# An attention-decode backward kernel: dV written over V, one buffer for dK, V loaded one turn earlier

## The chip, the cores and the metric

The kernel runs on one core of one Trainium2 chip. The metric is device time in microseconds (us) for one execution, the median of several runs; lower is better. The profile is one execution recorded by the hardware profiler. Its engines are PE (TensorE matmul; PEld is its weight load), DVE (VectorE), ACT (ScalarE), POOL (GpSimd) and SP (SyncE, which here only issues DMA transfers). L645 is line 645 of the kernel.

## What is computed

The reference mixes two branches by a gate and returns the output and the gradients of nine inputs. Almost all bytes belong to the first branch, one decode step of attention with 32 heads, 4096 cached keys and a head size of 128:

```python
q = (x @ wq).reshape(B, Sq, H, Dh).transpose(0, 2, 1, 3)
scores = einsum("bhqd,bhkd->bhqk", q, k_cache) * Dh ** -0.5
o = einsum("bhqk,bhkd->bhqd", softmax(scores), v_cache)
a = o.transpose(0, 2, 1, 3).reshape(B, Sq, H * Dh) @ wo
h = einsum("bsd,df->bsf", x, w1) + b1          # second branch
b = einsum("bsf,fd->bsd", h * tanh(softplus(h)), w2)
out = g * a + (1 - g) * b                      # g = sigmoid(sum(x * gate_w))
```

With one query per head, dV of a head is the outer product of its probabilities and of dO, and dK the outer product of dscores and of q. So K and V (33.6 MB each, bf16) are read once, and dK and dV, as large, are written once. wq, wo, w1, w2 and their gradients are much smaller.

## The kernel before

Two heads make a pair; there are NP = 16 pairs and 8 groups of two pairs. One pair's K, V, dK or dV is one tile of 128 partitions x 64 rows x 128 values in bf16, 2048 KB, 16 KB in each partition. Buffers hold 2 K tiles and 2 V tiles (pool `kv_in`) and 2 output tiles `o_sb` (pool `outs`), which dV and dK share in turn.

The main loop (L882 to L974) makes turn i, for i = 0 to 14; turn 15 stands behind it, written out. The order of instructions is written by hand, each engine runs its own list in that order, and waits between engines follow from the tiles' uses, by the parts of a tile that are touched. Turn i does two things, interleaved:

- *Outputs of pair i.* `softmax` (a PE transpose to `mx`, L610, and a maximum), `exps` on ACT (L620), `pjs` on DVE (L624), a small PE product with the sums (`zd_mm`, L628), `probs` on DVE (L632 to L642: p, ds, and their masked copies pm, dsm). Then `dq_o` (L681) has PE read K(i) and V(i) for dq and o. `dv_out` and `dk_out` write dV(i) and dK(i) in four quarters each on DVE (L645, `outer`); the store is issued on SP's queue after the last quarter (L666), or in halves in turns 0 and 15 (L664).
- *Scores of pair i+1.* PE transposes K(i+1) and V(i+1) in eight pieces each (`k_pe`, `v_pe`, L549), ACT copies each piece out of PSUM (`ev`, L560), PE multiplies by q and dO (`k_rows`, `v_rows`, L575), and `rw_cp` (L586), `x_tr` (L592), `sels` (L599) and `maxes` (L604, L606) bring the scores into the form that the next turn's softmax reads. `k_pe(i + 1, 0)` to `(i + 1, 2)` stand ahead of `zd_mm(i)` in PE's list.

SP issues in its list's order, and an issue that has to wait holds up those behind it. In turn i these are: K(i+2) and V(i+2) right after `dq_o(i)` (L917, L918); dV(i)'s store; in odd turns weights for a later group (L935, L937); in even turns the stores of dwo and dwq of the group before (L424, L415); dK(i)'s store. A load waits until the tile that last used its buffer has been read.

Other work is put between these steps by `side(at, i, g, hp)` at named places `do("mx")`, `do("e")` and so on. In even turns (hp = 0) it does the sums of the group before: `f_diag` (DVE, L329 and L310), `f_o4` and `f_bc` (PE, L339 and L316), `l_pe` (L388), `l_add` (L394), `f_dx` (DVE, L400) and `f_dwq` (DVE, L410) for three columns at "dv" and two at "dk0", and `f_dwo` (ACT, L418). `mlp` puts in pieces of the second branch. In turn 14 dK is written into a free `Kn` buffer, in turn 15 dV into a free `Vn` buffer (L655, L657). After turn 15's outputs DVE, PE and ACT make three rows of small outputs (`vec_rows`, L1043), which POOL stores.

Of the kernel before, what the change touches and what calls it, by code (L numbers as in the profile page):

```python
# [16 lines left out]
def kernel(  # L17
# [25 lines left out]
    P = 128  # L43
# [45 lines left out]
    out9_rows = out_9.rearrange("(c p) -> c p", p=P)  # L89

    const = ctx.enter_context(tc.tile_pool(name="const", bufs=1))
    KBUFS, VBUFS = 2, 2
    kv_in = ctx.enter_context(tc.tile_pool(name="kv_in", bufs=KBUFS))
    kvT = ctx.enter_context(tc.tile_pool(name="kvT", bufs=1))
    outs = ctx.enter_context(tc.tile_pool(name="outs", bufs=2))
    wts = ctx.enter_context(tc.tile_pool(name="wts", bufs=3))
    grp_sb = ctx.enter_context(tc.tile_pool(name="grp_sb", bufs=2))
    small = ctx.enter_context(tc.tile_pool(name="small", bufs=3))
# [6 lines left out]

    def load(tiles, src, name, i, parts=1):
        if i < NP:
            tiles[i] = kv_in.tile([P, J, Dh], BF16, name=name, tag=name)
            for k in range(parts):
                yield nc.sync.dma_start(tiles[i][:, k * J // parts:(k + 1) * J // parts, :],  # L110
                                        src[i][:, k * J // parts:(k + 1) * J // parts, :])
# [4 lines left out]
    def load_v(i):  # L116
        return list(load(vts, Vv, "Vn", i))
# [6 lines left out]
    def load_wqp(k):  # L124
        a, z = WQP[k]
        wqp[k] = wts.tile([P, RC, (z - a) * GD], BF16, name="wq_p", tag="wq_p", bufs=2)
        for g in range(a, z):
            wqs[g] = wqp[k][:, :, (g - a) * GD:(g - a + 1) * GD]
        nc.sync.dma_start(wqp[k][:], wq_v[:, :, a * GD:z * GD])
# [20 lines left out]
    load_v(1)  # L150
    w1_sb = const.tile([P, RC, F], BF16, name="w1_sb")
    nc.sync.dma_start(w1_sb[:], w1_v)
    load_wqp(1)
    load_wo(2)
    w2_sb = const.tile([P, FCN, D], BF16, name="w2_sb")
# [235 lines left out]
    def l_add(g, slot, o):  # L391
        ax = groups[g]["ax"]
        if o:
            nc.vector.tensor_tensor(aT_acc[:], aT_acc[:], ax[:, 0, :], ALU.add)  # L394
        if ("q", g) in wT:
            nc.vector.tensor_copy(dx_parts[:, :, slot], ax[:, 1, :])
# [26 lines left out]
    def f_dwo_st(g):  # L423
        nc.sync.dma_start(dwo4_v[g], wos[g][:])  # L424
# [227 lines left out]
    def out_part(w, i, dst, col4, row, k):  # L652
        if k == 0:
            if w == "k" and i == NP - 2:
                o_t[w, i] = kv_in.tile([P, J, Dh], BF16, name="Kn", tag="Kn")  # L655
            elif w == "v" and i == NP - 1:
                o_t[w, i] = kv_in.tile([P, J, Dh], BF16, name="Vn", tag="Vn")  # L657
            else:
                o_t[w, i] = outs.tile([P, J, Dh], BF16, name="o_sb", tag="o_sb")
        outer(o_t[w, i], col4, row[:, i % 2 * Dh:(i % 2 + 1) * Dh], k * JQ, (k + 1) * JQ)  # L660
        if i in (0, NP - 1):
            if k % 2:
                js = slice((k - 1) * JQ, (k + 1) * JQ)
                nc.sync.dma_start(dst[i][:, js, :], o_t[w, i][:, js, :])  # L664
        elif k == 3:
            nc.sync.dma_start(dst[i], o_t.pop((w, i))[:])  # L666

    def dv_out(i, k):
        out_part("v", i, dVv, p4s[i], groups[i // 2]["do_row"], k)
# [3 lines left out]
            out_part("k", i, dKv, ds4s[i], groups[i // 2]["qs_row"], k)  # L673

    def dq_o(i):
        K, V = kts.pop(i), vts.pop(i)
        for r in range(J // 8):
            for c in range(4):
                N, m = (K, dsmb) if c < 2 else (V, pmb)
                jb = 4 * (2 * r + c % 2)  # L680
                nc.tensor.matmul(rw[32 * c:32 * c + 8, :], lhsT=m[:, jb:jb + 4, :].rearrange("p q a -> p (q a)"),  # L681
                                 rhs=N[:, jb:jb + 4, :].rearrange("p j d -> p (j d)"),
                                 start=(i == NP - 1 and r == 0), stop=(i == NP - 1 and r == J // 8 - 1))
# [132 lines left out]
    def side(at, i, g, hp):  # L816
        nx, pv = g + 1 < NG, g > 0
        if hp == 0 and pv:
            f = g - 1
            if at == "probs":  # L820
                f_new(f)
                f_diag(f)
            if at == "dqo":
                f_o4(f)
                f_bc(f)
                f_o4c(f)
            if at in ("v2", "v3", "v4", "v5"):
                f_dwo(f, int(at[1]) - 2)
            if at == "k7":
                l_pe(f, 0, G)  # L830
            if at == "v5":
                f_dwo_st(f)
            if at == "dv":
                l_add(f, f, True)
                for c in range(3):
                    f_dx(f, c)
                    f_dwq(f, c)
            if at == "dk0":
                for c in range(3, RC):
                    f_dx(f, c)  # L840
                    f_dwq(f, c)
                f_dwq_st(f)
        if hp == 0:
            kind, gw = ("o", g + 1) if nx else ("q", g)
            if at == "v3":
                w_pe(kind, gw, 0)
                ev()
            if at == "vr":
                w_pe(kind, gw, 1)
                ev()  # L850
            if at == "v7":
                w_pe(kind, gw, 2)
                ev()
        if hp == 0 and nx:
            if at == "v7":
                g_new(g + 1)
                g_q(g + 1)
            if at == "x":
                g_qcol(g + 1)
                g_do(g + 1)  # L860
        if hp == 1 and nx:
            if at == "mx":
                g_qpair(g + 1)
            if at == "k1":
                g_qpair_cp(g + 1)
                g_docol(g + 1)
            if at == "k3":
                g_dopair(g + 1)
            if at == "dv":
                g_qs(g + 1)  # L870
            if at == "probs":
                g_dopair_cp(g + 1)
        if hp == 1 and at in ("dv", "v3", "dk0"):
            mlp(i, 2.0)
        elif at == "e" or hp == 1 and at == "k3":
            mlp(i, 1.0, ("act", "dh", "dx", "dw1"))
        elif at == ("v7", "dk1")[hp]:
            mlp(i, 0.9 + 0.9 * hp, ("h", "b1", "b", "diag", "bc"))
        if i >= 1 and at in (("k7", "v2", "v3", "v4", "v5", "v7") if hp == 1 else ("k7", "v7")):
            dw2_some(1)  # L880

    for i in range(NP - 1):  # L882
        g, hp = i // 2, i % 2

        def do(at):
            side(at, i, g, hp)

        if i == NP - 2:
            assert not mq
            nc.sync.dma_start(dw1_v[:, 0:3, :], w1_sb[:, 0:3, :])  # L890
            nc.sync.dma_start(dw1_v[:, 3:RC, :], w1_sb[:, 3:RC, :])
        mx, negM = softmax(i)
        do("mx")
        k_pe(i + 1, 0)
        k_pe(i + 1, 1)
        ev()
        dqo_red(i - 1, xs[i])
        exps(i, negM)
        do("e")
        ev()  # L900
        do("k1")
        k_pe(i + 1, 2)
        ev()
        pjs(i)
        zd_mm(i, mx)
        k_pe(i + 1, 3)
        ev()
        do("k3")
        probs(i, mx)
        do("probs")  # L910
        k_pe(i + 1, 4)
        k_pe(i + 1, 5)
        k_rows(i + 1, 0)
        ev()
        ev()
        dq_o(i)
        load_k(i + 2)  # L917
        load_v(i + 2)  # L918
        if i == NP - 2:
            assert dw2_next[0] == FCN  # L920
            m_dw2(0)
            dw2_store()
            nc.gpsimd.dma_start(db1_row, dh_bc[0:1, :])
        do("dqo")
        dv_out(i, 0)
        dv_out(i, 1)
        k_pe(i + 1, 6)
        ev()
        k_pe(i + 1, 7)
        ev()  # L930
        do("k7")
        dv_out(i, 2)
        dv_out(i, 3)
        if hp == 1 and 0 < g and g + 2 < NG:
            load_wo(g + 2)  # L935
        if hp == 1 and g % 2 == 0 and g > 0 and g + 4 <= NG:
            load_wqp(g // 2 + 1)  # L937
        do("dv")
        v_pe(i + 1, 0)
        v_pe(i + 1, 1)  # L940
        k_rows(i + 1, 1)
        ev()
        ev()
        v_pe(i + 1, 2)
        ev()
        do("v2")
        v_pe(i + 1, 3)
        ev()
        do("v3")
        v_pe(i + 1, 4)  # L950
        v_pe(i + 1, 5)
        v_rows(i + 1, 0)
        ev()
        do("v4")
        ev()
        do("vr")
        dk_out(i, 0)
        do("dk0")
        v_pe(i + 1, 6)
        ev()  # L960
        do("v5")
        v_pe(i + 1, 7)
        ev()
        do("v7")
        dk_out(i, 1)
        do("dk1")
        v_rows(i + 1, 1)
        rw_cp(i + 1)
        x_tr(i + 1)
        dk_out(i, 2)  # L970
        dk_out(i, 3)
        sels(i + 1)
        maxes(i + 1)
        do("x")  # L974
# [102 lines left out]
```

## Time and profile before

| | |
|---|---|
| median of 3 runs | 404.15 us (403.64 to 405.39) |
| the profiled execution | 403.98 us, of which 402.2 us from the first to the last instruction (the span) |
| DVE, PE, ACT busy | 279.4, 292.4, 226.2 us (69%, 73%, 56% of the span) |
| bytes moved | 164.54 MB, half read and half written |
| K's loads, issue to landing, median | 13.7 us |
| V's loads, issue to landing, median | 18.3 us |
| stores of o_sb, issue to landing, median | 16.6 us |

In the profile's groups of instructions the columns are: line, engine, operation, tiles, shapes and count, then busy us, mean ns of one, idle us just before them and what ended it. The slices cut the span in 40 equal parts; a digit is the busy share in tenths. The lists in order of time give the start, the length, the engine and the line.

### The profile page before, as it was taken

What the parts mean: (1) busy time and instruction counts of PE and PEld (TensorE: products, weight loads), DVE (VectorE), ACT (ScalarE), POOL (GpSimd) and SP (SyncE); (2) the same over time, 40 slices, a digit from 0 to 9 for tenths busy, and PEclk for the clock granted to TensorE, in tenths of its full rate; (3) what the DMA queues carried; (4) which work ended last, traced back from release to release, by engine and by line L of the source; (5) the groups of instructions that cost most, each with busy time, mean ns of one, the idle gap of its engine ahead of it and who ended that gap; (6) DMA issues with size and microseconds to landing.
All of it is one profiled execution on the core that took longest, in us unless ns stands there. A gap on an engine that the chain in (4) does not pass through costs nothing.

```text
span 402.2 us, 7414 instructions
## 1 busy us (share of the span) xinstructions
PE 292.4 (73%) x2886; PEld 207.5 (52%) x2886; DVE 279.4 (69%) x696; ACT 226.2 (56%) x484; POOL 25.5 (6%) x50
## 2 busy tenths in 40 slices
PE   3788888886968696984939886695967879197530
PEld 3557654665645474754627563553735655074320
DVE  2206537587966996478798956767496897859890
ACT  3464756485557544583535858377486885168130
POOL 9200005100000000000000004000000000010001
PEclk9898999898999888797977999599698999779555
DMA  7999999999999999999999999999999999999996
GB/s 273 432 423 413 416 420 431 424 427 423 403 402 425 432 419 424 404 429 430 424 433 400 380 408 431 428 423 425 418 406 383 419 376 427 433 417 430 412 407 234
DMA packets 20115, 164.54 MB, mean 409 GB/s; under 512 B 2455, under 2 KB 2456, under 8 KB 10904
## 3 DMA queue, kind: packets, MB, share of 16 engines
q1 hardware_dynamic: 18960, 159.62, 96.1%
q0 software_dynamic: 1088, 4.44, 2.7%
q8 instruction: 22, 0.36, 0.3%
q14 instruction: 13, 0.11, 0.1%
q10 hardware_dynamic: 32, 0.01, 0.0%
HBM read 82.44 MB, written 82.44 MB: 410 GB/s over the span
## 4 chain that ended last, share of the span: by engine, by line
DMA 62%; DVE 26%; PE 6%; issue 2%; ACT 2%; POOL 0%; POOLq 0%; DVEq 0%; ACTq 0%
DMA out_dram<-o_sb 60%; DVE o_sb L645 18%; PE tr L549 3%; DVE junk L400 2%; DMA Kn<-in_A_k_cache_dram 1%; DVE Kn L645 1%; DVE Vn L645 1%; DVE wq_p L410 1%; ACT T L560 1%; PE rw L575 1%; DVE ds L637 0%; PE q_ps L246 0%; PE mx L610 0%; DVE wo_g L421 0%; PE do_ps L301 0%
## 5 line engine op out<-in xcount | busy, mean ns | idle before, releaser
L560 ACT COPY T<-tr 128x512 f32<-128x512 f32 x256 | 140.9, 592 | 115.8 <-PE tr L549 67.6
L549 PE MATMUL tr<-ident_f,Kn 128*128 128x128 f32 x512 | 89.9, 338 | 7.6 <-DMA Kn<-in_A_k_cache_dram 7.6
L645 DVE TENSOR_TENSOR o_sb<-do_row,p 128x2048 bf16<-128x2048 bf16 x60 | 69.5, 1220 | 32.1 <-DMA out_dram<-o_sb 32.1
L549 PE MATMUL tr<-ident_f,Vn 128*128 128x128 f32 x512 | 77.2, 284 | 12.6 <-ACT T L560 12.6
L549 PEld LDWEIGHTS tr<-ident_f,Kn 128*128 128x128 f32 x512 | 78.4, 181 | 14.0 <-issue 9.8
L645 DVE TENSOR_TENSOR o_sb<-qs_row,ds 128x2048 bf16<-128x2048 bf16 x60 | 71.3, 1235 | 11.5 <-DMA out_dram<-o_sb 11.5
L549 PEld LDWEIGHTS tr<-ident_f,Vn 128*128 128x128 f32 x512 | 54.1, 140 | 37.1 <-ACT T L560 22.8
L610 PE MATMUL mx<-ident_f,m_s 128*128 128x128 f32 x16 | 6.8, 427 | 36.9 <-DVE m_s L606 36.9
L681 PE MATMUL rw<-Kn,dsm 128*8 128x512 bf16 x256 | 31.9, 394 | 1.2 <-DVE dsm L641 1.1
L681 PE MATMUL rw<-Vn,pm 128*8 128x512 bf16 x256 | 31.9, 394 | 0.0
L575 PE MATMUL rw<-T,doz 128*32 128x512 bf16 x256 | 20.3, 392 | 14.3 <-ACT T L560 14.3
L400 DVE SCALAR_TENSOR_TENSOR junk<-wq_p,dq_bc 128x512 bf16<-128x512 bf16 x35 | 24.0, 685 | 0.0
L610 PEld LDWEIGHTS mx<-ident_f,m_s 128*128 128x128 f32 x16 | 2.7, 167 | 41.2 <-DVE m_s L606 41.2
L418 ACT ACTIVATE wo_g<-da_bc,o 128x640 bf16<-128x640 bf16 x28 | 23.8, 849 | 0.0
L592 PE MATMUL x<-ident_f,rw_sb 128*128 128x128 f32 x68 | 12.2, 306 | 13.7 <-ACT rw_sb L586 13.7
L575 PE MATMUL rw<-T,qz 128*32 128x512 bf16 x256 | 20.8, 400 | 0.4 <-ACT T L560 0.4
L592 PEld LDWEIGHTS x<-ident_f,rw_sb 128*128 128x128 f32 x68 | 7.7, 149 | 22.8 <-ACT rw_sb L586 22.8
L681 PEld LDWEIGHTS <-dsm 128*8 128x8 bf16 x256 | 11.5, 88 | 14.0 <-DVE dsm L641 2.5
L604 DVE TENSOR_REDUCE m<-sd 128x1 f32<-128x64 f32 x16 | 3.4, 215 | 18.0 <-ACT sd L599 18.0
L586 ACT COPY rw_sb<-rw 128x512 f32<-128x512 f32 x17 | 10.0, 590 | 10.4 <-PE rw L575 5.6
L575 PEld LDWEIGHTS <-doz 128*32 128x32 bf16 x256 | 5.4, 94 | 19.6 <-issue 19.4
L599 ACT COPY sd<-x 64x128 f32<-64x128 f32 x32 | 8.3, 260 | 12.7 <-PE x L592 7.3
(183 smaller groups left out, 358.5 us busy)
## 6 DMA issues: line engine op xcount, KB each, us to landing
out_dram<-o_sb SPq DMA_DIRECT2D x27, 2048.0 KB, 16.6
Kn<-in_A_k_cache_dram SPq DMA_DIRECT2D x15, 2048.0 KB, 13.7
Vn<-in_A_v_cache_dram SPq DMA_DIRECT2D x15, 2048.0 KB, 18.3
out_dram<-o_sb SPq DMA_DIRECT2D x6, 1024.0 KB, 13.5
wq_p<-in_A_wq_dram SPq DMA_DIRECT2D x4, 1280.0 KB, 24.9
wo_g<-in_A_wo_dram SPq DMA_DIRECT2D x8, 640.0 KB, 21.0
out_dram<-wo_g SPq DMA_DIRECT2D x8, 640.0 KB, 13.2
out_dram<-wq_p SPq DMA_DIRECT2D x4, 1280.0 KB, 14.7
```

The source lines that it names most:

```text
L400: nc.vector.scalar_tensor_tensor(jq[:], in0=wqs[g][:, c, :], scalar=1.0, in1=groups[g]["dq_bc"][:], op0=ALU.mult, op1=ALU.mult, accum_out= ...
L410: nc.vector.tensor_scalar(wqs[g][:, c, cs], groups[g]["dq_bc"][:, cs], x_col_f[:, c:c + 1], None, ALU.mult)
L418: nc.scalar.activation(wos[g][:, hh, :], da_bc[:], ACT.Copy, scale=groups[g]["o4"][:, hh:hh + 1])
L549: nc.tensor.transpose(tp[:, t, :], words[:, t * P:(t + 1) * P], ident_f[:])
L560: nc.scalar.copy(TT[w, i, k][:, (3 - c) * (TB // 2):(4 - c) * (TB // 2), :], tp[:])
L575: nc.tensor.matmul(rw[32 * c:32 * (c + 1), :], lhsT=z[:, at:at + 32], rhs=Tb[:, c, par, :, :], start=first and par == 0, stop=last and par ...
L586: nc.scalar.copy(rw_sb[i][:].rearrange("p t r -> p (t r)"), rw[:])
L592: nc.tensor.transpose(xs[i][:, 3 - j, :], t[:, j, :], ident_f[:])
L599: nc.scalar.copy(sd[i][hs].rearrange("p s (k j) -> p k s j", k=2), v[hs, :, 8 + 4 * a:12 + 4 * a].rearrange("p j (k s) -> p k s j", k=2))
L610: nc.tensor.transpose(mx[:, 0:P], dgms.pop(i)[:].to_broadcast([P, P]), ident_f[:])
L645: nc.vector.tensor_tensor(dst[:, a:b, :].rearrange("p j (k t) -> p j k t", t=4), row.rearrange("p (k t) -> p k t", t=4).unsqueeze(1).to_br ...
L681: nc.tensor.matmul(rw[32 * c:32 * c + 8, :], lhsT=m[:, jb:jb + 4, :].rearrange("p q a -> p (q a)"), rhs=N[:, jb:jb + 4, :].rearrange("p j ...
```

## The change

Three V buffers instead of two, one `o_sb` buffer instead of two. dV(i) is written into V(i)'s own tile and stored from there; `o_sb` is left to dK (in turn 14 a Kn buffer, as before). V(i+3) instead of V(i+2) is loaded in turn i, at its end behind dK's store; V(2) is loaded in the prologue. In even turns the group's `f_diag` moves from "probs" to "e", `f_o4` and `f_bc` from "dqo" to "k3"; the place "dv" (three columns of `f_dx` and `f_dwq`, `g_qs`, and `mlp` in odd turns) moves ahead of `dv_out`, `l_add` gets a place of its own, "la", and "dk0" moves ahead of dK's first quarter. `mlp`'s small pieces swap places "e" and "k3".

```diff
-    KBUFS, VBUFS = 2, 2
+    KBUFS, VBUFS = 2, 3
...
-    outs = ctx.enter_context(tc.tile_pool(name="outs", bufs=2))
+    outs = ctx.enter_context(tc.tile_pool(name="outs", bufs=1))
...
-            tiles[i] = kv_in.tile([P, J, Dh], BF16, name=name, tag=name)
+            tiles[i] = kv_in.tile([P, J, Dh], BF16, name=name, tag=name, bufs=KBUFS if name == "Kn" else VBUFS)
...
     nc.sync.dma_start(w1_sb[:], w1_v)
+    load_v(2)
     load_wqp(1)
...
             if w == "k" and i == NP - 2:
-                o_t[w, i] = kv_in.tile([P, J, Dh], BF16, name="Kn", tag="Kn")
-            elif w == "v" and i == NP - 1:
-                o_t[w, i] = kv_in.tile([P, J, Dh], BF16, name="Vn", tag="Vn")
+                o_t[w, i] = kv_in.tile([P, J, Dh], BF16, name="Kn", tag="Kn", bufs=KBUFS)
+            elif w == "v":
+                o_t[w, i] = vts.pop(i)
             else:
                 o_t[w, i] = outs.tile([P, J, Dh], BF16, name="o_sb", tag="o_sb")
...
     def dq_o(i):
-        K, V = kts.pop(i), vts.pop(i)
+        K, V = kts.pop(i), vts[i]
...
-            if at == "probs":
+            if at == "e":
                 f_new(f)
                 f_diag(f)
-            if at == "dqo":
+            if at == "k3":
                 f_o4(f)
                 f_bc(f)
                 f_o4c(f)
...
+            if at == "la":
+                l_add(f, f, True)
             if at == "dv":
-                l_add(f, f, True)
                 for c in range(3):
                     f_dx(f, c)
                     f_dwq(f, c)
...
-        elif at == "e" or hp == 1 and at == "k3":
+        elif at == "k3" or hp == 1 and at == "e":
             mlp(i, 1.0, ("act", "dh", "dx", "dw1"))
...
         dq_o(i)
         load_k(i + 2)
-        load_v(i + 2)
...
         do("dqo")
+        do("dv")
         dv_out(i, 0)
         dv_out(i, 1)
...
-        do("dv")
+        do("la")
         v_pe(i + 1, 0)
...
         do("vr")
+        do("dk0")
         dk_out(i, 0)
-        do("dk0")
...
         dk_out(i, 3)
+        load_v(i + 3)
         sels(i + 1)
         maxes(i + 1)
```

## The prediction, made before the changed kernel was run

> **What bounds the kernel.** I read the page's slices first, then the waits, then time-ordered lists of the last three turns. A turn i is one pass of the main loop: the softmax and the outputs of pair i, and the transposes of pair i+1.
>
> From the page:
> ```profile
> DMA  7999999999999999999999999999999999999996
> GB/s 273 432 423 413 416 420 431 424 427 423 403 402 425 432 419 424 404 429 430 424 433 400 380 408 431 428 423 425 418 406 383 419 376 427 433 417 430 412 407 234
> DMA packets 20115, 164.54 MB, mean 409 GB/s; under 512 B 2455, under 2 KB 2456, under 8 KB 10904
> ```
> All slices but the first and last have the DMA engines busy 90% or more, and all but three of those move 400 to 433 GB/s. 164.54 MB at 430 GB/s are 382.7 us of a 402.2 us span. The 19.5 us of difference lie at the ends (270 GB/s in the first 10 us: 3.7; the last 12 us, at 321 and less: 4.7), in rates just under 430, and in dips: the 10 us stretches from 100, 110, 220, 230, 290, 300 and 320 moved 400, 402, 398, 374, 406, 369 and 385 GB/s, together 6.4 us short of 430. In the dips the engines are still busy:
> ```profile
> 230.00:240.00 10.00, 8.15 (x100) 5.47 (x97) 5.52 (x23) 6.78 (x18) 0.00 (x0) 1.00 0.95 374
> 300.00:310.00 10.00, 6.02 (x45) 4.95 (x45) 6.81 (x18) 6.80 (x15) 0.00 (x0) 0.83 0.99 369
> 380.00:390.00 10.00, 5.52 (x63) 3.21 (x53) 9.97 (x21) 3.22 (x9) 0.00 (x0) 0.50 0.95 396
> ```
> (The last two columns are the busy share and GB/s; the columns in front are PE, PEld, DVE, ACT, POOL and PE's clock.) A share of 0.99 at 369 GB/s means slow packets, not a lack of work. So DVE's waits for stores cost little:
> ```profile
> L645 DVE TENSOR_TENSOR o_sb<-do_row,p 128x2048 bf16<-128x2048 bf16 x60 | 69.5, 1220 | 32.1 <-DMA out_dram<-o_sb 32.1
> L645 DVE TENSOR_TENSOR o_sb<-qs_row,ds 128x2048 bf16<-128x2048 bf16 x60 | 71.3, 1235 | 11.5 <-DMA out_dram<-o_sb 11.5
> ```
> DVE stands still because the queue ahead of it is full; the chain of waits gives `out_dram<-o_sb` 60% for the same reason. **DMA is the bound in the middle, and only at the end does computing catch up with it.**
>
> The Trainium skill, HBM Reference, Specifications, says that a core streaming alone reaches about 425 GB/s and is bounded by its DMA engines. By that the bytes need 387.2 us instead of 382.7, with 15 us around them instead of 19.5; the trace passes it (439 GB/s in 340 to 350), and either way the rule speaks against a gain from fewer waits.
>
> **The change, part by part.** Bytes and DMA counts stay as they are: 16 loads each of K and V, the same stores. DVE, ACT and PE run the same instructions.
>
> *dV in V's buffer.* DVE no longer waits for an older store before dV: the 32.1 us go. What is late next in a turn is K. V(i+2) now stands in front of K(i+2) instead of behind it. A 2048 KB transfer takes 4.9 us (K(15) landed 15.6 us after its issue at 334.56, V(15) 20.0 after 334.99: 350.1 and 355.0). So K(i+2) lands 4.9 us later against the same stream of bytes. PE's transposes of K stand ahead of the small product for the softmax's sums (L628), so a late K holds back the probabilities and all behind them. I expect every turn from the second on to start its PE work when K lands.
>
> *Does DMA then run dry?* Count from k, the landing of the K that turn j transposes, by distances of turn 14 (first transpose 352.25, probabilities done 357.2, Kn's and Vn's reads done about 359.4). Turn j issues K(j+2) at k+7.3, dV(j) at about k+12.7 (4.9 to the probabilities, 3.0 of group sums, 4.6 of dV), dK(j) at k+20.7 or before. The queue after k holds dV(j-1) 4.9, weights 1.5 to 4.6, dK(j-1) 4.9, V(j+2) 4.9: 16.2 us before K(j+2) is needed, 21.1 before dV(j), 27.5 before dK(j). Margins: 8.9, 8.4, 6.8 us. V(j+2) has to wait on SP until dV(j-1), whose buffer it takes, has landed at k+4.9; 6.4 us are then still queued. Queued on SP behind that wait are K's load and dV's store, both later anyway. An issue costs at most 3.0 us before its data flow (first load: 1024 KB issued at 0.81, landed 5.40 later, 2.4 of it the transfer). **Cost in the middle: 0**, and the cover is those margins of 3.4 us and more.
>
> SP's own waits in the profile show where such a wait is spent: SP stood 80.8 us before loads of line 110 until PE had read the buffer (line 681). The Trainium skill, DMA: Bandwidth & Descriptors, Anatomy of one DMA, says the same in general: DMA engines wait for no semaphore, the sequencer that issues does. By that V's wait holds up everything that SP issues next, which is the third rival below; by the margins it costs nothing.
>
> *One buffer for dK.* dK(j) may start when dK(j-1) has landed, k+11.3 to k+14.4; DVE reaches it at k+13 to k+16. Nothing to a few tenths; covered by the 6.8 us. The last one, dK(15), comes two turns after the buffer was last used and doesn't wait.
>
> *Group sums in the softmax.* The 3.0 us of sums (three pairs of 0.62 and 0.35 us in the chain) now stand before dV instead of after it, in even turns: dV is later, dK not. The two small PE products (o_ps and bc_ps, 0.46 us in all behind dq_o) go ahead of the probabilities: up to 0.5 us gained in the PE chain of an even turn.
>
> *V(2) in the first loads.* K(2) lands 4.9 us later; in the first 60 us the queue only gets fuller (K(2) was issued at 38.8 and the loads before it landed until 47.3). 0.
>
> **The end is another matter.** After K(15) no load is left, and the stores of turn 15 depend on a chain from K(15)'s transposes to the last small outputs:
> ```profile
> 352.25 2.77 PE L549 MATMUL tr<-ident_f,Kn 128*128 128x128 f32 x12
> ...
> 374.81 0.47 PE L610 MATMUL mx<-ident_f,m_s 128*128 128x128 f32 x1 [1.46 <-DVE m_s L606]
> ...
> 379.43 0.64 PE L681 MATMUL rw<-Vn,pm 128*8 128x512 bf16 x2
> ```
> ```profile
> 373.39 0.53 ACT L599 COPY sd<-x 64x128 f32<-64x128 f32 x2 [0.74 <-PE x L592]
> ```
> ```profile
> 378.91 1.22 DVE L645 TENSOR_TENSOR Vn<-do_row,p 128x2048 bf16<-128x2048 bf16 x1
> ```
> ```profile
> SPq L1072 <- DMA out_dram<-vec_rows: 5.2, 1, 5.2
> ```
> 1. *K(15).* Its landing moves from 350.1 to V(15)'s old place, 355.0, and the transposes from 352.25 to about 355.15: +2.9. The chain to `sd` (ends 373.9) is PE and ACT, nearly without slack; less the 0.5 above, +2.4 (bounds: 0, if the chain has slack that I don't see, to 2.9).
> 2. *dV(15).* It was written into a free Vn buffer at 378.91, while PE still read V(15). Now it is V(15)'s own: DVE must wait until PE has read that quarter. Stores of parts of o_sb are issued while DVE writes the next part (39.73, with DVE working to 45.6), so waits go by parts; the first quarter's last read ends at 380.07: +1.2 (all of V: 382.6, +3.7). In earlier turns this wait falls under the group sums or where DMA has margin.
> 3. *Last outputs.* SP's last long wait is for the three small stores of `vec_rows`, issued at 394.15 to 395.49 and landed 5.0 us later (median), with 2 us to the span's end. They hang on DVE's last chain and move by all of 1 and 2. I take back 0.4, since they then meet less traffic (bounds 0 to 0.7, the median's 5.0 against the 5.7 of the first one). The large stores have some 2 us of room of their own (the first half of dK(15) landed 5.7 us after its issue, 2.4 of it transfer, and at most 3.0 around it), so they end before that.
>
> Sum: 2.4 + 1.2 - 0.4 = **+3.2**, on the profiled execution's 403.98 (span 402.2, 1.8 around it): **407.2 us**. The median of the runs, 404.15, is 0.2 above that execution; I don't add it. By the bounds: 0 + 1.2 - 0.7 = +0.5 to 2.9 + 3.7 = +6.6, so 404.5 to 410.6.
>
> **Rivals.**
> - *The end is absorbed, 404 to 405 (0.25).* Dips and the chain's slack vary; if K(15) comes early against the computing, step 1 is 0 and step 2 is hidden by large stores that end last anyway (+0.5). For it: 0.5 us lie between the two ends now. Against: PE's waits in that turn, 0.1 to 1.3 us each, are for ACT, which was itself busy.
> - *Store waits were the bound, 399 (0.15).* If the dips come from the order of loads and stores, new order may end them: 6.4 us less, with the end's 3.2 still paid or not: 397.6 to 400.8. For it: the chain's 60%. Against: busy share 0.99 in the dips; loads and stores still alternate in pairs.
> - *SP's wait starves the queue, 410 (0.12), slower.* V(i+3) waits for the slowest engine's part of dV(i): the 16 engines finished V(15) between 349.7 and 355.0. An engine 5.3 us ahead has 6.4 - 5.3 = 1.1 us queued when V is issued, against up to 3.0 until data flow: up to 1.9 idle us per turn. It decides once the leading engines' idle time exceeds what they are ahead; about 0.25 us in each of 13 turns is 3 us more: 410. Against: the slowest engine, which sets landings, keeps its queue.
> - That the change doesn't do what it says: only if K were not late, which is the first rival.
>
> **Chances.** Forecast, 405.5 to 409: 0.48. The first rival lies within 0.5% of 404.15 (2.0 us, about what a measurement of this kernel can tell), the second below, the third above; of the forecast's own span the lowest part is within. Faster 0.15, same 0.28, slower 0.57. Range 401.5 to 410.5, which leaves out most of the second rival and half of the third, together under 0.2.
>
> **What would show it.** Right: DVE's wait before dV nearly gone; PE waits for Kn of some us in most turns; K(15) lands after the softmax of turn 14 has begun; the Vn form of line 645 waits for PE line 681 in turn 15; DMA share near 1.00 until about 385. Wrong: shares below 0.95 in the middle (starved), GB/s near 430 without dips (faster), or the first transpose of K(15) within 1 us of the start of turn 14's softmax (absorbed).

## The result, and the profile after

Over 18 runs each, the changed kernel takes 406.62 us (median; 404.68 to 411.39) and the kernel before 404.15 us (401.57 to 406.41). One run of the changed kernel, the one of 411.39 us, was in a slower state that some executions show, and the ratio leaves it out. The ratio is 1.0067, 95% interval 1.0045 to 1.0088: +2.7 us, between +1.8 and +3.6. The profiled execution of the changed kernel took 406.48 us with a span of 404.7 us, against 403.98 and 402.2 before. From line 153 on, the changed kernel's lines that are named here stand one further down than before (L645 is now L646); those behind the main loop stand three further down (L1072 is now L1075).

The page's slices of the changed kernel, and its chain by engine:

```profile
DMA  8999999999999999999999999999999999999886
GB/s 273 433 421 422 407 424 423 420 421 420 427 395 435 422 424 424 416 432 422 421 398 422 411 416 417 384 427 434 387 398 406 400 389 436 429 413 432 364 373 243
DMA packets 20115, 164.54 MB, mean 407 GB/s; under 512 B 2455, under 2 KB 2456, under 8 KB 10904
```
```profile
PE 39%; DMA 34%; ACT 15%; DVE 8%; issue 2%; POOL 0%; POOLq 0%; ACTq 0%; DVEq 0%
```
The bytes are the same. The last three slices fall to 8, 8 and 6, where before only the last one was under 9: the end has grown. In between the share stays at 9, but the dips are still there (395, 384, 387, 389 GB/s). The groups show where the waits went:

```profile
L550 PE MATMUL tr<-ident_f,Kn 128*128 128x128 f32 x512 | 89.2, 333 | 29.4 <-DMA Kn<-in_A_k_cache_dram 29.4
L646 DVE TENSOR_TENSOR Vn<-do_row,p 128x2048 bf16<-128x2048 bf16 x64 | 74.1, 1218 | 4.8 <-PE rw L682 4.8
L646 DVE TENSOR_TENSOR o_sb<-qs_row,ds 128x2048 bf16<-128x2048 bf16 x60 | 70.4, 1231 | 1.8 <-DMA out_dram<-o_sb 1.8
```
DVE's two waits for stores, 32.1 and 11.5 us before, are 0 and 1.8 us. In their place PE waits 29.4 us for K. The lists of waits of all engines and of SP's queue (us in total, times, longest) have one that has grown, shown first as it was before and then as it is now, and one that is new, V's load on SP:

```profile
DVE pj L624 <- ACT e_bf L620: 10.1, 11, 2.1
```
```profile
DVE pj L625 <- ACT e_bf L621: 30.0, 11, 7.9
```
```profile
SPq L110 <- DMA out_dram<-Vn: 106.7, 13, 15.4
SPq L1075 <- DMA out_dram<-vec_rows: 6.2, 1, 6.2
```
The first is K's lateness again: ACT's exponentials of turn i stand in ACT's list behind the copy of K(i+1)'s first piece, so a late K holds up the softmax too. The new one stands until dV has left V's buffer. The wait for the last small outputs, listed behind it, was 5.2 us before.

The end, in PE's and DVE's lists in order of time:

```profile
352.28 0.48 PE L611 MATMUL mx<-ident_f,m_s 128*128 128x128 f32 x1 [4.00 <-DVE m_s L607]
354.64 2.79 PE L550 MATMUL tr<-ident_f,Kn 128*128 128x128 f32 x12 [1.89 <-DMA Kn<-in_A_k_cache_dram]
...
376.76 0.47 PE L611 MATMUL mx<-ident_f,m_s 128*128 128x128 f32 x1 [1.07 <-DVE m_s L607]
```
```profile
382.05 2.36 DVE L646 TENSOR_TENSOR Vn<-do_row,p 128x2048 bf16<-128x2048 bf16 x2 [1.12 <-PE rw L682]
```
K(15) is transposed from 354.64 (before 352.25), the softmax of turn 15 starts at 376.76 (374.81), dV(15) at 382.05 (378.91).

### The profile page after: what moved, and what is told of

Same layout as the page of the kernel before. It is cut to its first block, busy times and chain, and to the rows that moved or that the text cites. A ratio compares the mean times of both kernels' runs of the same rounds, so it can differ in the third digit from the quotient of the medians.

```text
span 404.7 us, 7415 instructions
## 1 busy us (share of the span) xinstructions
PE 292.9 (72%) x2886; PEld 205.1 (51%) x2886; DVE 278.9 (69%) x696; ACT 227.0 (56%) x484; POOL 29.5 (7%) x50
## 4 chain that ended last, share of the span: by engine, by line
PE 39%; DMA 34%; ACT 15%; DVE 8%; issue 2%; POOL 0%; POOLq 0%; ACTq 0%; DVEq 0%
DMA Kn<-in_A_k_cache_dram 34%; PE tr L550 19%; ACT T L561 7%; PE rw L682 7%; PE rw L576 6%; ACT wo_g L419 3%; PE x L593 1%; ACT rw_sb L587 1%; DVE Vn L646 1%; PE mx L629 1%; DVE o_sb L646 1%; ACT sd L600 1%; PE h_ps L446 1%; PE mx L611 1%; ACT w_sb L538 1%
## 5 line engine op out<-in xcount | busy, mean ns | idle before, releaser
L550 PE MATMUL tr<-ident_f,Kn 128*128 128x128 f32 x512 | 89.2, 333 | 29.4 <-DMA Kn<-in_A_k_cache_dram 29.4
L550 PEld LDWEIGHTS tr<-ident_f,Kn 128*128 128x128 f32 x512 | 75.7, 177 | 40.7 <-issue 23.1
L550 PE MATMUL tr<-ident_f,Vn 128*128 128x128 f32 x512 | 77.2, 283 | 12.7 <-ACT T L561 12.7
L646 DVE TENSOR_TENSOR Vn<-do_row,p 128x2048 bf16<-128x2048 bf16 x64 | 74.1, 1218 | 4.8 <-PE rw L682 4.8
L646 DVE TENSOR_TENSOR o_sb<-qs_row,ds 128x2048 bf16<-128x2048 bf16 x60 | 70.4, 1231 | 1.8 <-DMA out_dram<-o_sb 1.8
L625 DVE SCALAR_TENSOR_TENSOR pj<-sd,e_bf 128x64 f32<-128x64 f32 x16 | 3.6, 223 | 30.3 <-ACT e_bf L621 30.0
L593 PE MATMUL x<-ident_f,rw_sb 128*128 128x128 f32 x68 | 12.7, 315 | 12.6 <-ACT rw_sb L587 12.6
L517 POOL TENSOR_TENSOR mjunk<-ident_bf,dh_bf 128x96 bf16<-128x96 bf16 (+4 forms) x9 | 8.2, 943 | 171.4 <-DVE dh_bf L514 171.4
L682 PEld LDWEIGHTS <-dsm 128*8 128x8 bf16 x256 | 11.2, 88 | 14.7 <-DVE dsm L642 5.6
L509 DVE SCALAR_TENSOR_TENSOR junk<-w_sb,dm,db_bc 128x640 bf16<-128x640 bf16 x16 | 14.1, 881 | 4.8 <-PE bc_ps L317 4.6
## 6 DMA issues: line engine op xcount, KB each, us to landing
out_dram<-o_sb SPq DMA_DIRECT2D x13, 2048.0 KB, 14.7
```

Of the source, the lines that this page charges most:

```text
L509: nc.vector.scalar_tensor_tensor(junk[:], in0=w2_sb[:, fc, :], scalar=dm[:, fc:fc + 1], in1=db_bc[:], op0=ALU.mult, op1=ALU.mult, accum_ou ...
L517: nc.gpsimd.tensor_tensor(mjunk[:, i * FCN:(i + n) * FCN].rearrange("p (a b) -> p a b", b=FCN), ident_bf[:, a:b].unsqueeze(2).to_broadcast ...
L550: nc.tensor.transpose(tp[:, t, :], words[:, t * P:(t + 1) * P], ident_f[:])
L593: nc.tensor.transpose(xs[i][:, 3 - j, :], t[:, j, :], ident_f[:])
L646: nc.vector.tensor_tensor(dst[:, a:b, :].rearrange("p j (k t) -> p j k t", t=4), row.rearrange("p (k t) -> p k t", t=4).unsqueeze(1).to_br ...
```

## The experiments

The theory at first: the end costs some 3 us, in the two steps of the prediction, and the middle nothing. The rivals: the middle pays or gains too, with terms that hide one another. All kernels were timed against the kernel before; "us" below is the ratio less 1, times 404.15. "End" is the span less the landing of the last load of K or V, in the profiled execution. "Idle" and "slow" are DMA time in us of 16 engines between 20 and 375 us, worked out from the trace's packets. Idle counts, at each moment, how many packets fewer than 16 are under way, as a share of 16. Slow is the time that packets took over what their size usually takes (0.611 us for 16 KB).

| kernel | ratio, 95% interval | us | end | idle | slow |
|---|---|---|---|---|---|
| before | 1 | 0 | 47.2 | 0.90 | 8.5 |
| after | 1.0067 (1.0045 to 1.0088) | +2.7 | 50.2 | 1.51 | 8.5 |
| e1: after, V(15) behind K(15) | 0.9977 (0.9944 to 1.001) | -0.9 | 48.6 | 0.70 | 6.9 |
| e2: after, dV(15) in a free buffer | 0.9997 (0.9966 to 1.0028) | -0.1 | 48.4 | 0.30 | 6.4 |
| e3: after, both | 0.9974 (0.9942 to 1.0005) | -1.1 | 47.4 | 0.52 | 8.0 |
| e7: before, dV(15) over V(15) | 1.0012 (0.9986 to 1.0037) | +0.5 | 47.8 | 0.59 | 7.3 |
| e8: before, V(15) ahead of K(15) | 1.0047 (1.0025 to 1.0069) | +1.9 | 49.4 | 1.15 | 7.7 |
| e4: before, V(i+2) ahead of K(i+2) | 1.0248 (1.02 to 1.0295) | +10.0 | 49.9 | 3.58 | 13.3 |
| e5: before, moved places alone | 0.9921 (0.9894 to 0.9948) | -3.2 | 46.8 | 0.62 | 7.1 |
| e6: before, V(i+2) behind dV(i)'s store | 0.9931 (0.9903 to 0.996) | -2.8 | | 0.14 | 6.3 |
| e10: e5 and e6 together | 0.9937 (0.9906 to 0.9969) | -2.5 | | 0.05 | 5.7 |
| e12: before, buffers alone | 0.996 (0.9929 to 0.9991) | -1.6 | 48.1 | 0.73 | 6.6 |
| e11: buffers and moved places | 0.9861 (0.9818 to 0.9904) | -5.6 | 47.8 | 0.14 | 5.5 |
| e9: buffers and V a turn ahead, no moves | 1.0038 (1.0009 to 1.0067) | +1.5 | 50.8 | 0.72 | 7.9 |

In e6 and e10 dV(13)'s store stands between K(15) and V(15), so their end isn't comparable and is left out. The last three columns come from one profiled execution of each kernel, and idle and slow scatter: e2 differs from the changed kernel, and e7 from the kernel before, in turn 15 alone, which begins near 375 us, and yet idle and slow together are 6.7 against 10.0 us and 7.9 against 9.4. A difference of 2 or 3 us in these two columns shows nothing by itself.

**The end, undone in the changed kernel: e1, e2, e3.**

```diff
         load_k(i + 2)
+        if i == NP - 3:               # e1, e3
+            load_v(i + 2)
...
-        load_v(i + 3)
+        if i != NP - 4:               # e1, e3
+            load_v(i + 3)
...
+            elif w == "v" and i == NP - 1:      # e2, e3
+                o_t[w, i] = kv_in.tile([P, J, Dh], BF16, name="Vn", tag="Vn", bufs=VBUFS)
             elif w == "v":
                 o_t[w, i] = vts.pop(i)
```


> The changed kernel, with the last V load (pair 15) moved from the end of turn 12 to right behind the load of K(15) in turn 13; nothing else. Theory 1 (the loss is in the chain from K(15) to the last small outputs): K(15) lands some 4.9 us earlier (about 349.6 instead of 354.5), its first transpose follows turn 14's softmax at once (about 352.3 instead of 354.6), turn 15's softmax begins near 374.6 instead of 376.55, and the time falls by about 2.0 us, 406.6 to 404.6. Rival (the queue is starved in the middle by V's wait on SP): that wait is still there in twelve turns, so the time stays near 406.6.

> The changed kernel, with dV of the last pair written into a free V buffer instead of over V(15). Theory 1: dV(15)'s first quarter begins when the probabilities are done, without the 1.1 us wait for line 682 (PE), and the time falls by 1.2 us, 406.6 to 405.4. Rival (the last large stores end the kernel and hide it): no change, 406.6.

> The changed kernel with both edits: K(15) loaded ahead of V(15), and dV(15) in a free V buffer. Theory 1: both losses at the end go, 3.1 us, 406.6 to 403.5, within 0.3% of the kernel before, since DMA sets the pace in the middle of both. Rival (starved queue): 406.6. Rival (DVE's store waits had been worth something and the end hid it): clearly below the kernel before, 402 or less.

Medians: 404.48, 404.14 and 403.27 us, so 2.1, 2.5 and 3.4 us less than the changed kernel; by the ratios in the table it is 3.6, 2.8 and 3.8 us. e1 and e3 came out as theory 1 had it, and e2 gained twice the 1.2 us that were expected. All three intervals lie below the changed kernel's, but they overlap one another, so the times show that the end costs some 3 to 4 us but don't tell its two steps apart. The end of the span does, in one execution each: 50.2 with both steps, 48.6 and 48.4 with one, 47.4 with none, against 47.2 before. In e3 K(15) no longer waits for its landing:

```profile
349.82 0.48 PE L611 MATMUL mx<-ident_f,m_s 128*128 128x128 f32 x1 [3.59 <-DVE m_s L607]
350.09 2.77 PE L550 MATMUL tr<-ident_f,Kn 128*128 128x128 f32 x12
```
**The same two steps, put into the kernel before: e7, e8.**

```diff
-                o_t[w, i] = kv_in.tile([P, J, Dh], BF16, name="Vn", tag="Vn")      # e7
+                o_t[w, i] = vts[i]
...
-        K, V = kts.pop(i), vts.pop(i)      # e7
+        K, V = kts.pop(i), vts[i]
...
+        if i == NP - 3:               # e8
+            load_v(i + 2)
         load_k(i + 2)
-        load_v(i + 2)
+        if i != NP - 3:
+            load_v(i + 2)
```


> The kernel before with dV of the last pair alone written over V(15). Theory 1: DVE waits about 1.1 us for line 681 (PE) before dV(15), the last small outputs come as much later, and from the landing of the last load to the span's end it is 48.3 us instead of 47.2; the time rises by about 1.2 us, 404.3 to 405.5. Rival (the last large stores hide it): no change.

> The kernel before with V(15) loaded ahead of K(15), the other pairs as before. Theory 1: K(15)'s landing moves from 350.1 to about 355, PE's chain of turn 14 starts 2 to 2.5 us later, turn 15 begins as much later; from the landing of the last load to the span's end 49.2 to 49.7 us instead of 47.2; the time rises by 2.0 to 2.4 us, 404.3 to about 406.5. The 10.5 us of the run with V first in every turn were then mostly a queue run short in the middle, which this kernel can't have. Rival (late K costs by itself wherever it is): as theory 1 here, so this run tells only the end's part.

Measured 404.25 and 406.18 us. e8's time is what was expected, though K(15)'s transposes start only 1.4 us later than before; its PE list shows the wait that e3 lost:

```profile
350.47 0.47 PE L610 MATMUL mx<-ident_f,m_s 128*128 128x128 f32 x1 [7.26 <-DVE m_s L606]
353.61 2.79 PE L549 MATMUL tr<-ident_f,Kn 128*128 128x128 f32 x12 [2.67 <-DMA Kn<-in_A_k_cache_dram]
```
e7's +0.5 us is within its interval of nothing; in the trace the end is 0.6 us longer, half of the 1.2 us that were expected. So both steps of the end stand in the traces, from both sides: K(15) last costs 1.0 to 2.2 us of the end (e2 and e8 against before, e1 against the changed kernel, e3 against e2), dV(15)'s wait 0.6 to 1.8 us (e7 and e1 against before, e2 against the changed kernel, e3 against e1; also e11 against e5, and e12 against before). In times, e8 shows the first by itself in the kernel before; the second alone is not shown there (e7).

**The middle: order of loads and moved places in the kernel before: e4, e5, e6.** e5 takes over the moves of `side` and of the three `do` lines as in the change's diff, and nothing else.

```diff
-        load_k(i + 2)                 # e4
         load_v(i + 2)
+        load_k(i + 2)
...
-        load_v(i + 2)                 # e6: behind the issue of dV(i)'s store
...
+        load_v(i + 2)
```


> The kernel before, with one edit: in each turn V(i+2) is loaded ahead of K(i+2) instead of behind it. Buffers, waits on stores and the places of the sums are as before. Theory 1: K lands 4.9 us later in each turn, which the middle hides, and K(15) lands near 355.0, so that PE's chain of turn 14 starts 2.4 us later: 404.15 to about 406.5. Rival (the new buffers or V's wait on SP cost the time): no change, 404.15.

> The kernel before with the moved places alone (group sums at e and k3, the place dv ahead of dV, dk0 ahead of dK, l_add behind dV, mlp's places swapped); buffers and loads as before. Theory 1: the moves cost nothing, since DVE waits there for stores anyway and DMA sets the pace: 404.3, within 0.3%. Rival (moving 3 us of sums ahead of dV in even turns makes dV's store late and the queue short): some tenths to 1 us per even turn from the second, up to 7 us, 411.

> The kernel before with one edit: V(i+2)'s load is issued behind dV(i)'s store instead of right behind K(i+2)'s load, so that loads and stores alternate one by one instead of in pairs. K(15) keeps its place. Theory 1 (the middle is set by bytes; slow packets come whatever the order): 404.3 within 0.4%. Rival (the dips in the DMA rate come from the order of loads and stores): the slow packets change clearly, 2 us or more either way.

Theory 1 missed in all three: 414.86, 400.77 and 401.52 us. For e6 the rival fits: the slow time falls by 2.2 us (8.5 to 6.3) and the run by 2.8, so the order of loads and stores among themselves is worth something, though the slow time of single executions scatters as much. V ahead of K, with the old buffers, costs 10.0 us, only some 2.7 of them at the end (49.9 against 47.2). The DMA engines run dry there, which slices of a fortieth hide and a window of 4 us shows (last two columns: busy share, GB/s):

```profile
64.00:68.00 4.00, 4.00 (x41) 1.97 (x34) 3.94 (x5) 2.30 (x5) 0.00 (x0) 1.00 0.77 250
86.00:90.00 4.00, 3.91 (x61) 2.95 (x55) 4.00 (x4) 2.14 (x6) 0.00 (x0) 1.00 0.86 320
```
PE and DVE work all the time in these windows; they are late, and the issues that hang on them too: SP issued nothing from 45.8 to 65.3 us, 19.5 us, where the same pause in the kernel before was 12.7. K's lateness shows in PE's waits for it, 32.3 us in this kernel (7.6 before). The moves alone, which the prediction had at about nothing, gain 3.2 us. With that the theory of an untouched middle had fallen: after both steps of the end are undone the changed kernel is at -1.1 (e3), 2 us slower than its own moves alone (e5).

**Which part of the change costs what in the middle: e9, e11, e12, and e10.**

```diff
-    load_v(2)                         # e11
...
         load_k(i + 2)
+        load_v(i + 2)                 # e11
...
-        load_v(i + 3)                 # e11
```
e9 is the changed kernel with the moved places put back, e12 has both edits (so buffers alone), and e10 is e5 and e6 together.

> The changed kernel with the group sums and the other moved instructions back where they stood before; buffers and loads as changed. My theory: the moves gain by filling DVE's waits for stores, which the changed kernel doesn't have, so without them only the 0.5 us of PE's chain comes back: about 407.1 (ratio to before about 1.007). Rival: the moves are worth the 3.1 us that they gained in the kernel before wherever they stand, and buffers and load order alone cost 5 to 6 us: about 409.7 (ratio about 1.014).

> The kernel before with the moved places and with the load of V(i+2) behind the store of dV(i), buffers as before: the two edits that gained 3.1 and 2.6 us alone. My theory: both take away the same thing, queues that run short, so together they gain little more than one: 399.5 to 401 us. Rival: the gains add up: about 398.4 us.

> The changed kernel with V(i+2) loaded right behind K(i+2) in the same turn, as before the change; dV over V, three V buffers, one dK buffer and the moved places stay. My theory: K is first again, so the end costs only dV(15)'s wait for V(15)'s reads (about 1 us) on top of the 400.8 us of the moves alone: about 401.8. Rival: the one dK buffer or dV over V costs in the middle, whatever the loads' order: 404 or more.

> The kernel before with the buffers of the change alone: three V buffers, one for dK, dV over V; loads and places as before. Known so far: before 404.3, moves alone 400.8, buffers and moves 399.6, all of the change 406.6 us. My theory: DVE's waits before dV go with the buffers, and the moves gained by filling these waits, so without the waits the moves are worth little: buffers alone stand near buffers and moves, about 400.5 us (ratio to before 0.991). Rival: the moves gain the same 3 us with any buffers while K is loaded first, and the buffers are worth only the 1.2 us between 400.8 and 399.6: about 403 us (ratio 0.997).

Medians: e9 406.1, e10 401.6, e11 399.58, e12 402.4 us. The kernel before, the change and four of these make a table of two by three (us against before):

| | places as before | places moved |
|---|---|---|
| buffers as before, V behind K | 0 | -3.2 (e5) |
| new buffers, V behind K | -1.6 (e12) | -5.6 (e11) |
| new buffers, V a turn further ahead | +1.5 (e9) | +2.7 (the change) |

Read downward, the load order costs 3.1 us without and 8.3 us with the moves (between 0.7 and 5.6 us, and between 5.7 and 11 us, from the ends of the intervals), of which the traces put about 2.5 at the end (50.8 against 48.1; 50.2 against 47.8). Read across, the moves gain 3.2 and 4.0 us where V stands behind K, and nothing where it stands ahead (+1.5 and +2.7, with intervals that overlap). e9 bears out the theory that the moves bring the changed kernel little: its ratio of 1.0038 lies nearer to the theory's 1.007, which is just outside its interval, than to the rival's 1.014. e12 throws out the theory's reason. The moves don't gain by filling DVE's waits for dV's stores: e12 has none of these, only 33.9 us before dK, of which e11 keeps 32.9, and yet the moves gain 4.0 us between the two. Nor is it DVE's wait before dV for PE's reads of V: the moves shorten it from 10.2 to 4.4 us with V behind K (e12, e11), and by more, from 13.1 to 4.8, where they gain nothing (e9, the changed kernel). So for e12 the rival's 403 fits and my 400.5 doesn't; e11 came 2.2 us under my 401.8 and further from its rival. e10 came 0.6 us above my range: two edits that gain 3.2 and 2.8 alone gain 2.5 together, so they don't add up.

e11 is the fastest kernel, 1.4% under before (1.0% to 1.8%); its interval and e5's share only the stretch from 0.9894 to 0.9904. What the load order does on SP's queue is seen in the lists of issues. First the changed kernel around a dry spell, SP's issues and a window:

```profile
273.05 0.34 SPq L667 DMA_DIRECT2D out_dram<-Vn  x1
278.52 0.34 SPq L425 DMA_DIRECT2D out_dram<-wo_g  x1
279.96 0.33 SPq L667 DMA_DIRECT2D out_dram<-o_sb  x1
291.52 0.34 SPq L110 DMA_DIRECT2D Vn<-in_A_v_cache_dram  x1
294.11 0.34 SPq L110 DMA_DIRECT2D Kn<-in_A_k_cache_dram  x1
```
```profile
290.00:295.00 5.00, 4.62 (x56) 2.58 (x55) 3.90 (x10) 2.42 (x6) 0.00 (x0) 0.92 0.86 336
```
dK's store goes out at 279.96, and nothing follows for 11.6 us: V takes the buffer of the dV that was issued at 273.05 and waits until that has landed. From 290 to 295 the engines are busy 86% and move 336 GB/s. The trace's completion times of single engines show why: 15 of the 16 had finished that dV between 284.8 and 288.7, the last one only at 291.5. By then the first four were through with dK's store too (291.1 to 291.2) and had nothing left. But the spell isn't in every execution. e2 and e3 run the same instructions up to here, with the same pause (10.3 and 10.0 us) and 102.0 and 97.6 us of this wait on SP. Here are e2's issues and its window, and then e3's window:

```profile
277.73 0.42 SPq L669 DMA_DIRECT2D out_dram<-o_sb  x1
288.04 0.34 SPq L110 DMA_DIRECT2D Vn<-in_A_v_cache_dram  x1
```
```profile
290.00:295.00 5.00, 4.38 (x48) 2.60 (x36) 5.00 (x7) 3.87 (x9) 0.00 (x0) 1.00 1.00 419
```
```profile
290.00:295.00 5.00, 4.54 (x55) 2.49 (x54) 3.23 (x4) 2.56 (x6) 0.00 (x0) 0.94 1.00 416
```
In both the 16 engines finished that dV within 4.6 us of one another instead of 6.7, V was issued 1.8 us before the first of them was through with dK, and the share stayed at 1.00. So of these three executions the queue ran dry only in the one where an engine lagged. Now e11, where V takes a buffer whose store is a turn older: SP's waits, its issues in the same turns, the slices, and its window from 300 to 340 with that of the changed kernel behind it:

```profile
SPq L110 <- PE rw L681: 107.5, 13, 12.2
...
SPq L110 <- DMA out_dram<-Vn: 16.7, 11, 2.5
```
```profile
277.89 0.33 SPq L666 DMA_DIRECT2D out_dram<-o_sb  x1
286.72 0.34 SPq L110 DMA_DIRECT2D Kn<-in_A_k_cache_dram  x1
288.20 0.34 SPq L110 DMA_DIRECT2D Vn<-in_A_v_cache_dram  x1
```
```profile
DMA  7999999999999999999999999999999999999995
GB/s 271 431 420 419 417 417 429 429 407 413 431 418 426 427 417 430 410 431 430 426 427 426 430 408 439 416 423 430 424 406 420 423 397 436 419 414 432 397 398 226
```
```profile
300.00:340.00 40.00, 33.10 (x342) 23.12 (x341) 34.33 (x83) 27.09 (x59) 0.00 (x0) 0.94 1.01 420
```
```profile
300.00:340.00 40.00, 31.86 (x315) 22.43 (x315) 32.87 (x81) 27.67 (x59) 0.00 (x0) 0.87 1.00 400
```
The wait for dV's store falls from 106.7 to 16.7 us. SP still waits, but mostly for PE's reads (107.5 us, 38.1 in the changed kernel), so the two together fall only from 144.8 to 124.2. The idle time falls from 1.51 to 0.14 us. Between 300 and 340 the engines move 420 GB/s instead of 400, at a busy share of 1.00 and more in both: there the changed kernel lost by slow packets, not for lack of work, and e2 and e3 moved 418 and 421 in the same stretch. The queue is also longer: in the lists of DMA issues a store of dV takes 18.8 us from issue to landing in e11 and 15.0 us in the changed kernel (dK's: 18.4 and 14.7).

## Why the prediction was right, and where it was not

The time came out at 406.62 us for a forecast of 407.2, and the end is where the prediction put it. But its sum had one term for the end and nothing for the rest, and the nothing was two large terms that nearly cancel. That part of the agreement is luck.

- *K(15) lands in V(15)'s old place.* Right. It landed at 354.5 (predicted 355.0) and was transposed from 354.64 (355.15): +2.39 instead of +2.9, and the softmax of turn 15 moved by 1.95 (2.4). The size is a little less since the whole stream of loads ended 0.5 us sooner, at 354.5 instead of 355.0.
- *dV(15) waits for the reads of V(15).* Right: 1.12 us (predicted 1.2), by parts and not for all of V.
- *The last outputs move by all of it, less 0.4.* Right: dV(15) starts 3.14 us later, the first store of `vec_rows` is issued 3.16 us later (397.31 against 394.15), and the span grew by 2.5, so the take-back was 0.65. Undone, the end is worth 3.4 us by medians and 3.8 by ratios (e3 against the changed kernel), 2.8 in the traces, for a predicted 3.2.
- *Cost in the middle: 0, covered by margins of 3.4 us and more.* Wrong, though its count holds: it had 6.4 us queued behind V's wait, and at 291.5 dK's store was 6.3 us from landing. V's order costs 7.0 us between e11 and the changed kernel by the medians (399.58 and 406.62); with V(15) alone put back, 404.48, 4.9 us are left, which belong to the turns before the last K. The dry spell at 290 is what the prediction's third rival (SP's wait starves the queue) describes, and it took about 0.7 us (14% of 5 us). Between 20 and 375 us the changed kernel was idle for 1.4 us more than e11, and e2 for only 0.2 us more. So idle engines alone don't make up the 4.9 us; the rest of the difference between the traces of the changed kernel and e11 is slow packets (8.5 against 5.5), of which no run shows the cause.
- *Group sums: up to 0.5 us in an even turn's PE chain, dV later, dK not.* Wrong in size: the sum took 0.5 us once, at the end, and all moves together gain 3.2 us in the kernel before (e5).
- *dV in V's buffer, one buffer for dK: nothing to a few tenths.* Wrong in size: -1.6 us (e12), -0.4 to -2.9. With the moves it is -5.6 (e11).
- So the terms beside the end are about -5.6 for buffers and moves (e11), and +4.7 for V's order ahead of the last load (e1's -0.9 less e11's -5.6, between 1.6 and 7.8 by the ends of their intervals). e3, which has both and not the end, is at -1.1 (-2.3 to +0.2). The "0" was about right as a sum and not in these two parts. V(2) in the first loads was not tried by itself.
- *Store waits were the bound (the second rival).* Its time, 399, is what e11 reaches, with the same buffers and the same moves and without V's order. But the waits for stores weren't the reason as such: e12 takes away those before dV and gains 1.6 us, e5 leaves 23.3 of 32.1 us and gains twice that. The rival's other reason, that the dips come from the order of loads and stores, has e6 for it.
- *What would show it.* DVE's wait before dV is 4.8 us, all for PE. PE waited for K in 9 places, PE's weight loads in 4 more: most turns. The DMA share under 0.95 in a place of the middle, named as the sign of starving, was there, 0.86 at 290 to 295, in this execution and not in those of e2 and e3. The prediction's 439 GB/s in 340 to 350 counts a packet where it starts; with packets shared out over the windows that stretch moved 431, which still passes 425.

What stays open: how much of V's cost in the middle is V's wait for dV's store and how much K's lateness (e4 has the second alone and loses more than the change, with old buffers); and by which path the moves gain. In the profiled executions the moves shorten the span by 1.6 us with the old buffers (402.2 to 400.5) and by 2.0 with the new (401.1 to 399.1), half of what they gain by the ratios, and idle and slow DMA time together fall by about as much, 1.7 and 1.6 us (9.4 to 7.8, 7.3 to 5.7). That points at the DMA stream, but with a scatter of 2 to 3 us between executions of the same instructions it doesn't show it.

## What to carry to other kernels

In a kernel bound by its stream of bytes, the order of loads decides which one is late: put the load that the next step needs first in front, and count the last one at its full price. A load into a buffer that a store has to leave waits on the issuing queue for that store to land; look at what is left in the queue meanwhile, on the engine that is furthest ahead, and look in more than one execution: a dry spell in one trace need not be in the next. And a total that fits doesn't prove its terms: the parts of this change, taken one at a time, gave a kernel 7 us faster than the whole of it (medians of 399.58 and 406.62).

## What the runs showed of the hardware

- The 16 DMA engines aren't in step. They finished one 2048 KB load 5.3 us apart (V(15) of the kernel before, between 349.7 and 355.0), and a load of K at 267.77 in the changed kernel 6.7 us apart (279.9 to 286.6), 2.7 us of it one engine. So the landing time follows the last engine, while the first ones may be out of work, as at 291 in the changed kernel.
- Packets of 16 KB usually take 0.611 us, but 1 to 3% of them take 1.0 to 2.2 us. All that packets take over their usual time makes 5.5 to 13.3 us of all engines' time between 20 and 375 us; four tenths to two thirds of it is in these long ones. They make the dips with a busy share near 1.00. Over the 14 kernels slow time goes with idle time: 5.5 to 6.4 us in the four kernels with 0.05 to 0.30 us idle, 13.3 in the one with 3.58. Which causes which wasn't tried.
- With almost no idle time between 20 and 375 us (0.14 us), e11 moved 422 GB/s. Its slices read up to 439, but they count a packet where it starts; with packets shared out, no stretch of 10 us passed 431. 16 engines with 16 KB each in 0.611 us are 429 GB/s. The Trainium skill, HBM Reference, Specifications, gives about 425 GB/s for a core that streams alone: the mean agrees, single stretches pass it by a little.
